# Two linear-attention and MLP layers on one core: the mask of K'V in pieces, b1 turned by DMA, and a new order of operations

## The chip, the cores and the metric

The kernel runs on one core of a Trainium2 chip. Its time is device time of one execution in microseconds (us). It was run 12 times; the median is compared. One execution was also recorded by the hardware profiler, and the profile and the trace are of that one. The engines are called as the profile calls them: PE (TensorE: matmuls; PEld are its weight loads), DVE (VectorE), ACT (ScalarE), POOL (GpSimd) and SP (SyncE, which here only issues DMAs).

## What is computed

x has 2048 tokens of width 512. Two kinds of block alternate, A, B, A, B, each fed with a layernorm of x and added to x; both A blocks share their weights, and so do both B blocks.

```python
def A(x, wqkv, wo):                  # linear attention, 32 heads of 16
    q, k, v = heads(x @ wqkv)
    phi = lambda t: where(t > 0, t + 1, exp(t)) + 1e-6
    kv  = einsum("bhsd,bhse->bhde", phi(k), v)
    z   = phi(k).sum(s)
    o   = einsum(phi(q), kv) / (einsum(phi(q), z) + 1e-6)
    return o @ wo

def B(x, w1, b1, w2, b2):            # MLP, 512 -> 1792 -> 512
    h = gelu(layernorm(x) @ w1 + b1)
    return h @ w2 + b2

for _ in range(2):
    x = x + A(layernorm(x), wqkv, wo)
    x = x + B(layernorm(x), w1, b1, w2, b2)
```

The layernorm has no scale or shift. Inputs, weights and the output are bf16; the kernel keeps x in fp32 in SBUF from the first residual add to the last.

## The kernel before

**Tiles.** The tokens are 16 tiles of 128, in 4 chunks of 4 tiles. A layer, counted from 0 to 1, is one A and one B block. An operation is named by its kind, its layer and its tile or chunk: K0_8 is the key matmul of tile 8 in layer 0.

**The stages of a layer.** For every tile, `norm` (L569) takes bn_stats and bn_aggr on DVE (L573, L575), the power -1/2 on POOL (L585) and the normalised y on DVE (L598) or on ACT (L593, after a small product on POOL, L590). y is turned, features to partitions, in one of two ways: `transpose` (L604) has SP issue one DMA transpose of the 128x512 tile (L608); `transpose_pe` (L612) makes four transposes on PE (L621) and a copy out of PSUM on ACT (L631). A table WAY says which tiles go which way; tiles that it doesn't name go by DMA, and the y of layer 1's attention always does.

`attn_k` (L663) makes K of a tile with four matmuls (L672), and `phi` (L639) its exp on ACT (L642), relu on ACT (L653), a min on DVE (L655), and the sum on DVE or POOL (L659); a second form leaves out the relu and takes a maximum on DVE from PSUM (L646, L648). `attn_q` does this for Q of a chunk (L690 by token, L703 by feature), four groups of four matmuls. `attn_z` (L710) sums phi(K) over tokens by 16 small matmuls (L718).

V is not computed. By associativity K'V = (K' y) wv, so the kernel forms G = y' phi(K), 512x512: in layer 0 held in four PSUM banks over all tiles (`attn_g_held`, L737), in layer 1 chunk by chunk and added up in SBUF by DVE (`attn_g_chunk`, L769, L776 to L782). Then `attn_kv` (L785), once in a layer, is the junction between the key side and the query side:

- KV: 16 matmuls of 128 columns give the four diagonal 128x128 pieces of K'V in one PSUM bank (L792), from the copies of G in gtb (L753 on DVE, L750 on ACT).
- the mask: DVE multiplies the whole 128x512 bank with a 0/1 mask of 16x16 blocks into kvb (L809).
- M: four matmuls, each of one 128-column piece of kvb with wo (L813), whose results are copied to gtb, again by L753 and L750. They carry o and wo at once.

`attn_den` (L817) makes the denominators by a matmul (D, L859) and ln and exp(-x) on ACT (L861, L863), and scales phi(Q) on DVE or POOL (L867). Chunks 2 and 3 of layer 1 do it by token instead: a row product (L835), a sum over heads (L838), a reciprocal (L843), the scaling (L847), and a DMA transpose (L851). `attn_out` (L874) multiplies with gtb (WO, L883) and adds the residual (RA, DVE, L888). `mlp_front` (L891) norms and turns the tile again and adds b2 to x ahead of time (L900). `mlp_up` (L904) computes 14 feature groups of the chunk (W1, L915), with gelu and the bias b1c on ACT (L921); chunk 0 in two halves of 256 columns. `mlp_down` (L926) makes a tile's 14 matmuls in two runs of 7 (W2, L953), and DVE adds it to x (RB, L959) or, in layer 1, into the output buffer (L963), which SP stores (L965). The last tile is stored in two halves (L940 to L947).

**b1.** b1 is loaded as 14 rows of 128 into b1r (L987); a matmul with the identity turns it (L1007), and ACT copies it into b1c, one column for each feature group (L1009).

**What sets the order.** There is no loop on the chip. Each operation is put into a graph with what it reads, writes and holds, a duration, and a priority: a base by chunk and stage, plus a shift for its group from the table SHIFT. A list scheduler (L111) then plays the graph: of the operations whose inputs are ready within a window, an engine takes the one with the smallest priority number. Its durations decide the order alone; what comes out is a fixed list of instructions for each engine, with semaphore waits between engines where they are needed (`assign_waits`, L292). An engine works its list strictly in order, so an instruction that waits holds up all behind it, and SP's list holds all DMA transposes and output stores. Where a gelu follows an exp or ln in ACT's list, or the other way round, ACT loads its function table anew (L1085).

**Buffers.** PSUM has eight banks, given out by class: up-projection h at most 3 at once, down-projection and WO (w) 2, K 2, Q 2, G, KV and M together (g) 2, transposes and z (t) 2, D (n) 1. A tile's bank is free again when its last reader is done. The weights wv and wo are loaded by POOL's queue after tile 0's transpose, w1 and w2 after the last transposes of layer 0.

Of the kernel before, what the change touches and what calls it, by code (L numbers as in the profile page):

```python
# [6 lines left out]
BF16 = mybir.dt.bfloat16  # L7
# [284 lines left out]
def assign_waits(graph, order, sems, dma_sems):  # L292
# [10 lines left out]
    while len(done) < total:  # L303
# [45 lines left out]
    N_HALF=1, N_K=2, N_Q=2, P_Z0=5.39, N_PB=1, N_PT=8, P_DEN=-48.34, P_A2=-5.06, P_W1=49.73, P_W2=87.05,  # L349
    P_K=33.61, P_G=135.4, P_Q=207.59, STEP=5.63, A1_Q=118.84, A1_STEP=1.49, N_H=3, N_N=1, GAP=12.11,  # L350
    TABLE_PENALTY=11.0, WINDOW=97.32,
    SHIFT={
        "B00_0": -63.5, "B00_1": -8.1, "B00_2": 7.3, "B00_3": -93.5, "B01": 60.2, "B02": 12.9, "B03": 195.1,
        "B10_0": 6.1, "B10_1": -62.8, "B10_2": -11.2, "B10_3": 31.6, "B11": 42.0, "B12": 48.9, "B13": -60.8,
        "D00": -42.5, "D01": 23.0, "D02": 55.4, "D03": 24.7, "D10": -118.7, "D11": -103.1, "D12": 76.7,
        "D13": 90.0, "G00_0": -130.5, "G00_1": 65.4, "G00_2": -14.1, "G00_3": -19.5, "G01_0": 15.9,
        "G01_1": 32.9, "G01_2": 2.4, "G01_3": -18.4, "G02_0": 89.2, "G02_1": 11.0, "G02_2": 152.3,
        "G02_3": -18.7, "G03_0": 58.4, "G03_1": 74.1, "G03_2": 101.0, "G03_3": 281.4, "G10": -248.4,
        "G11": 5.3, "G12": 7.7, "G13": -15.3, "K00_0": -188.0, "K00_1": -66.0, "K00_2": -160.3,
        "K00_3": -101.8, "K01_0": -46.3, "K01_1": -84.0, "K01_2": -197.2, "K01_3": -13.6, "K02_0": 7.6,  # L360
        "K02_1": 18.1, "K02_2": 72.9, "K02_3": 2.3, "K03_0": -251.2, "K03_1": 0.9, "K03_2": 2.8,
        "K03_3": 76.6, "K10": 72.4, "K11": 2.0, "K12": 63.8, "K13": -58.7, "N00_0": -106.8, "N00_1": -194.3,
        "N00_2": -80.9, "N00_3": -49.7, "N01_0": -228.4, "N01_1": -16.6, "N01_2": -83.5, "N01_3": -64.6,
        "N02_0": -10.3, "N02_1": -11.4, "N02_2": -8.6, "N02_3": -0.6, "N03_1": 96.6, "N03_2": -8.3,
        "N03_3": 103.1, "N10": 6.8, "N11": -48.1, "N12": -72.3, "N13": -200.4, "O00_0": -264.0, "O00_1": 4.0,
        "O00_2": 1.2, "O00_3": 41.0, "O01": -60.1, "O02": -3.5, "O03": 43.5, "O10_0": 86.0, "O10_1": -1.6,
        "O10_2": 9.3, "O10_3": -188.8, "O11": -55.5, "O12": 209.8, "O13": 11.7, "Q00": 5.8, "Q01": -60.9,
        "Q02": 42.5, "Q03": 86.6, "Q10": 16.5, "Q11": -39.1, "Q12": 237.5, "Q13": 105.1, "U00_0": -36.4,
        "U00_1": -3.8, "U01": 7.7, "U02": -47.6, "U03": -113.5, "U10_0": 2.5, "U10_1": -172.4, "U11": 40.1,
        "U12": -58.4, "U13": 102.3, "V0": 2.2, "V1": 30.4, "W00": 0.8, "W01": 86.3, "W02": 7.8, "W03": -45.0,  # L370
        "W10": -2.9, "W11": 295.4, "W12": 166.9, "W13": 260.2, "Z00": 6.3, "Z01": 37.9, "Z02": 87.6,
        "Z10": -7.3, "Z11": -9.0, "Z12": -118.0, "Z13": -122.1, "b1": 69.7,
    },
    WAY={
        "TA0_0": "pe", "TA0_1": "pe", "TA0_2": "pe", "TA0_3": "pe", "TA0_4": "pe", "TA0_5": "pe",
        "TA0_6": "pe", "TA0_7": "pe", "TB0_0": "dma", "TB0_1": "pe", "TB0_2": "dma", "TB0_3": "dma",
        "TB1_0": "pe", "TB1_1": "pe", "TB1_2": "dma", "TB1_3": "dma", "b20_0": "dve", "b20_1": "dve",
        "b20_10": "dve", "b20_11": "pool", "b20_12": "pool", "b20_13": "pool", "b20_15": "pool",
        "b20_2": "pool", "b20_3": "dve", "b20_4": "dve", "b20_5": "dve", "b20_6": "dve", "b20_7": "dve",
        "b20_8": "dve", "b20_9": "pool", "b21_0": "pool", "b21_1": "pool", "b21_10": "pool", "b21_11": "dve",  # L380
        "b21_12": "pool", "b21_13": "pool", "b21_14": "dve", "b21_15": "pool", "b21_2": "pool",
        "b21_3": "dve", "b21_4": "pool", "b21_5": "pool", "b21_6": "dve", "b21_7": "dve", "b21_8": "dve",
        "b21_9": "pool", "cpg0_0": "dve", "cpg0_1": "dve", "cpg0_2": "dve", "cpg0_3": "act", "cpg1_0": "act",
        "cpg1_1": "act", "cpg1_2": "act", "cpg1_3": "dve", "cpm0_0": "act", "cpm0_1": "dve", "cpm0_2": "dve",
        "cpm0_3": "act", "cpm1_0": "dve", "cpm1_1": "dve", "cpm1_2": "dve", "cpm1_3": "act", "den1_2": "tok",
        "den1_3": "tok", "normA0_0": "dve", "normA0_1": "dve", "normA0_10": "dve", "normA0_11": "act",
        "normA0_12": "dve", "normA0_13": "dve", "normA0_14": "dve", "normA0_15": "dve", "normA0_2": "dve",
        "normA0_3": "dve", "normA0_4": "dve", "normA0_5": "dve", "normA0_6": "dve", "normA0_7": "dve",
        "normA0_8": "dve", "normA0_9": "dve", "normA1_0": "act", "normA1_1": "dve", "normA1_10": "act",
        "normA1_11": "dve", "normA1_12": "dve", "normA1_13": "act", "normA1_14": "act", "normA1_15": "dve",  # L390
# [758 lines left out]
```

## Time and profile before

| what | value |
|---|---|
| median of 12 runs | 337.22 us (336.42 to 338.06) |
| the profiled execution's own time | 336.8 us |
| its span in the trace | 335.0 us |
| PE busy | 323.6 us, 1752 instructions |
| ACT busy | 222.8 us, 368 instructions |
| DVE busy | 203.0 us, 439 instructions |
| POOL busy | 140.0 us, 224 instructions |
| DMA transposes of y, issue to landing | 53, median 2.5 us |
| function table loads on ACT | 22 x 1.283 us |

The span is what the engines' records cover; the execution's own time is 1.8 us longer. A busy time is the union of an engine's records, so one matmul of 512 columns shows as 379 ns though the next one starts 216 ns after it. A group's line gives the source line, the engine, the operation and its shapes, the count, and after the bar the busy time and the mean of one in ns; after the second bar the time that the engine stood idle just before these instructions, and what ended most of it. The chain of work is followed back from the last instruction, each step to what released it.

### The profile page before, as it was taken

The numbers are of one execution on the slowest core, as the hardware profiler recorded it, in microseconds if no ns is written. First come the engines' busy times: TensorE is split into PE (matmuls) and PEld (weight loads), VectorE is DVE, ScalarE is ACT, GpSimd is POOL, SyncE is SP. The second block draws the span as 40 slices with busy tenths as digits, with TensorE's granted clock in tenths as the row PEclk, the third lists the DMA queues.
The fourth block names the chain that finished last, engine by engine and source line by source line (L and its number), as shares of the span: only waits on it lengthen the run. The fifth ranks groups of instructions, "written<-read, shape, count | busy, mean of one in ns | idle before, by whom it ended". The sixth has DMA issues, their size and how long they took to land.

```text
span 335.0 us, 4817 instructions
## 1 busy us (share of the span) xinstructions
PE 323.6 (97%) x1752; PEld 160.8 (48%) x1783; DVE 203.0 (61%) x439; ACT 222.8 (67%) x368; POOL 140.0 (42%) x224
## 2 busy tenths in 40 slices
PE   7889998999999999999999999999999999999996
PEld 2444443576444444444444444458644444444444
DVE  6987757985791017696305789699787593430122
ACT  3876899879569998642984398969916738327000
POOL 6653444466462012668303352678648271300000
PEclk9999999999999999999999999999999999999999
DMA  8733740022122000123200110003133412120011
GB/s 270 247 57 71 277 165 0 18 50 47 31 61 36 0 0 2 31 47 65 47 0 2 31 31 4 1 0 65 33 85 72 49 32 63 31 49 0 31 39 58
DMA packets 40068, 18.41 MB, mean 55 GB/s; under 512 B 33708, under 2 KB 39084, under 8 KB 40044
## 3 DMA queue, kind: packets, MB, share of 16 engines
q1 hardware_dynamic: 36476, 10.89, 15.7%
q0 software_dynamic: 1056, 4.72, 4.0%
q10 hardware_dynamic: 2512, 2.49, 2.3%
q8 instruction: 14, 0.23, 0.3%
q14 instruction: 10, 0.08, 0.1%
HBM read 8.00 MB, written 2.10 MB: 30 GB/s over the span
## 4 chain that ended last, share of the span: by engine, by line
PE 86%; DVE 6%; DMA 4%; POOL 1%; issue 1%; ACT 1%; POOLq 0%
PE ps L915 29%; PE ps L953 25%; PE ps L672 7%; PE ps L883 7%; PE ps L703 5%; PE ps L769 4%; PE ps L737 4%; DMA t<-yb 3%; PE ps L690 2%; DVE xsb L888 1%; PE ps L859 1%; DVE stats L573 1%; DMA t<-in_A_x_dram 1%; DVE gtb L753 1%; DVE yb L598 1%
## 5 line engine op out<-in xcount | busy, mean ns | idle before, releaser
L915 PE MATMUL ps<-t,w 128*128 128x512 bf16 (+1 forms) x555 | 99.5, 336 | 0.5 <-DMA t<-yb 0.3
L921 ACT ACTIVATE gT<-ps,b1c 128x512 bf16<-128x512 f32 (+1 forms) x140 | 79.3, 604 | 31.0 <-PE ps L915 30.8
L953 PE MATMUL ps<-w,gT 128*128 128x512 bf16 x424 | 96.9, 379 | 0.6
L915 PEld LDWEIGHTS ps<-t,w 128*128 128x128 bf16 x560 | 54.4, 98 | 43.9 <-DMA t<-yb 0.8
L953 PEld LDWEIGHTS ps<-w,gT 128*128 128x128 bf16 x434 | 42.2, 98 | 49.5
L642 ACT ACTIVATE eb<-ps 128x512 bf16<-128x512 f32 x64 | 38.6, 612 | 24.2 <-PE ps L672 16.1
L655 DVE TENSOR_SCALAR eb<-eb 128x512 bf16<-128x512 bf16 x56 | 18.2, 333 | 41.4 <-ACT eb L642 41.0
L585 POOL TENSOR_TENSOR rstd<-veps,neghalf 128x1 f32<-128x1 f32 x64 | 38.7, 605 | 7.2 <-DVE veps L583 2.1
L653 ACT ACTIVATE rb<-ps 128x512 bf16<-128x512 f32 x56 | 34.1, 616 | 0.0
L672 PE MATMUL ps<-wqkv,t 128*128 128x512 bf16 x123 | 31.3, 379 | 2.1 <-DMA t<-yb 1.8
L573 DVE BATCH_NORM_STATS2 stats<-xsb 128x6 f32<-128x512 f32 x48 | 32.6, 683 | 0.5
L883 PE MATMUL ps<-gtb,t 128*128 128x512 bf16 x123 | 30.8, 379 | 1.4 <-DVE gtb L753 1.0
L593 ACT ACTIVATE yb<-xsb,nmr,rstd 128x512 bf16<-128x512 f32 x20 | 16.2, 811 | 23.8 <-POOL nmr L590 23.0
L659 POOL TENSOR_TENSOR pkb<-eb,rb 128x512 bf16<-128x512 bf16 x11 | 12.8, 1170 | 35.9 <-ACT rb L653 18.3
L963 DVE TENSOR_TENSOR outb<-ps,xsb 128x512 bf16<-128x512 f32 x15 | 10.3, 684 | 28.7 <-PE ps L953 28.7
L1085 ACT ACT_TABLE_LOAD x21 | 26.9, 1283 | 0.4
L598 DVE TENSOR_SCALAR yb<-xsb,mv,rstd 128x512 bf16<-128x512 f32 x28 | 20.0, 717 | 8.5 <-POOL rstd L585 8.1
L867 POOL TENSOR_TENSOR t<-t,lr 128x512 bf16<-128x512 bf16 x14 | 16.3, 1165 | 20.6 <-ACT lr L863 20.5
L703 PE MATMUL ps<-t,wqkv 128*128 128x512 bf16 x92 | 23.1, 379 | 0.3
L900 POOL TENSOR_TENSOR xsb<-xsb,b2b 128x512 f32<-128x512 f32 x17 | 20.2, 1196 | 6.5 <-DVE yb L598 4.6
L883 PEld LDWEIGHTS ps<-gtb,t 128*128 128x128 bf16 x128 | 12.3, 98 | 16.7 <-DVE gtb L753 2.4
L672 PEld LDWEIGHTS ps<-wqkv,t 128*128 128x128 bf16 x128 | 12.0, 98 | 16.3 <-ACT rb L653 1.1
(82 smaller groups left out, 349.4 us busy)
## 6 DMA issues: line engine op xcount, KB each, us to landing
w<-in_B_w_dram POOLq DMA_DIRECT2D x4, 896.0 KB, 8.5
out_dram<-outb SPq DMA_DIRECT2D x15, 128.0 KB, 1.7
t<-in_A_x_dram ACTq DMA_DIRECT2D x3, 512.0 KB, 7.9
t<-yb SPq DMA_TRANSPOSE x53, 2.5
wqkv<-in_A_wqkv_dram SPq DMA_DIRECT2D x1, 512.0 KB, 5.2
wqkv<-in_A_wqkv_dram ACTq DMA_DIRECT2D x1, 512.0 KB, 7.0
wqkv<-in_A_wqkv_dram POOLq DMA_DIRECT2D x1, 512.0 KB, 6.8
wo<-in_A_wo_dram POOLq DMA_DIRECT2D x1, 512.0 KB, 6.3
```

The costliest lines, as they stand in the source:

```text
L573: G.op("dve", lambda e: e.bn_stats(stats[:, s.slot, :], src()), 620, reads=src_keys, writes=[k + "s"], tiles=[s, *src_tiles], prio=prio, n ...
L585: G.op("pool", lambda e: e.tensor_tensor(rstd[:, s.slot:s.slot + 1], veps[:, s.slot:s.slot + 1], neghalf[:], op=ALU.pow), 570, reads=[k + ...
L598: G.op("dve", lambda e: e.tensor_scalar(yb[:, y.slot, :], src(), mv[:, s.slot, 0:1], rstd[:, s.slot:s.slot + 1], op0=ALU.subtract, op1=ALU ...
L642: G.op("act", lambda e: e.activation(eb[:, et.slot, :], bank(bt), ACT.Exp), 478, reads=[src_key], writes=[f"e{tag}"], tiles=[bt, et], prio ...
L653: G.op("act", lambda e: e.activation(rb[:, rt.slot, :], bank(bt), ACT.Relu), 478, reads=[src_key], writes=[f"r{tag}"], tiles=[bt, rt], pri ...
L672: ins = e.matmul(bank(b), lhsT=yTa(yT)[:, dt, k * P:(k + 1) * P], rhs=wqkv[:, dt, D:2 * D], start=(dt == 0), stop=(dt == DT - 1))
L703: ins = e.matmul(bank(b), lhsT=wqkv[:, dt, kt * P:(kt + 1) * P], rhs=yTa(yT)[:, dt, :], start=(dt == 0), stop=(dt == DT - 1))
L883: ins = e.matmul(bank(wb), lhsT=yTa(pq)[:, kt, k * P:(k + 1) * P], rhs=gtb[:, kt, :], start=(kt == 0), stop=(kt == DT - 1))
L915: ins = e.matmul(bank(b, n), lhsT=w1[:, dt, ft * P:(ft + 1) * P], rhs=yTa(yT)[:, dt, k0 * P:k1 * P], start=(dt == 0), stop=(dt == DT - 1))
L921: G.op("act", lambda e, ft=ft, b=b, k0=k0, k1=k1, n=n: e.activation(gT[:, g.slot, ft * 512 + k0 * P:ft * 512 + k1 * P], bank(b, n), ACT.Ge ...
L953: ins = e.matmul(bank(b), lhsT=gT[:, g.slot, ft * 512 + k * P:ft * 512 + (k + 1) * P], rhs=w2[:, ft, :], start=(ft == 0), stop=(ft == FT - 1))
L1085: e.preload_act_table_set(sets[table])
```

## The change

Four edits:

1. `attn_kv` masks K'V in four instructions of 128 columns instead of one of 512, and each M matmul reads only its own piece.
2. b1 is turned by a DMA transpose that SP issues (from a 16-row b1r, which POOL clears first, into b1t) instead of a matmul; ACT then copies from b1t in SBUF instead of from PSUM. The transpose waits for b1's load and for the last transpose of layer 0.
3. A shift may be given to a single operation by its name, besides its group, and the tables of shifts and ways, the window, the penalty for a table change and the numbers of PSUM banks are new: K may hold 3 banks instead of 2, h 4 instead of 3, D 2 instead of 1. Of the transposes, tile 6 of layer 0 goes from PE to DMA and tile 11 from DMA to PE; of the MLP's, layer 0's tile 2 goes to PE and layer 1's tile 1 to DMA.
4. The scheduler's latency for a DMA transpose is 1300 instead of 1000; as every number of the scheduler it reaches the chip only through the order.

Entries of WAY whose names the program never asks for ("TA1_..", "tc_..") do nothing. The diff, with the tables cut to their first entries:

```diff
 CONF = dict(
-    N_HALF=1, N_K=2, N_Q=2, P_Z0=5.39, N_PB=1, N_PT=8, P_DEN=-48.34, P_A2=-5.06, P_W1=49.73, P_W2=87.05,
-    P_K=33.61, P_G=135.4, P_Q=207.59, STEP=5.63, A1_Q=118.84, A1_STEP=1.49, N_H=3, N_N=1, GAP=12.11,
-    TABLE_PENALTY=11.0, WINDOW=97.32,
+    N_HALF=1, N_K=3, N_Q=2, P_Z0=6.99, N_PB=1, N_PT=8, P_DEN=-45.12, P_A2=-16.36, P_W1=58.86, P_W2=84.95,
+    P_K=47.92, P_G=125.74, P_Q=226.77, STEP=5.92, A1_Q=51.41, A1_STEP=3.23, N_H=4, N_N=2, GAP=9.92,
+    TABLE_PENALTY=0.77, WINDOW=100.11,
     SHIFT={
-        "B00_0": -63.5, "B00_1": -8.1, "B00_2": 7.3, "B00_3": -93.5, "B01": 60.2, "B02": 12.9, "B03": 195.1,
+        "B00_0": -215.0, "B00_1": -89.8, "B00_2": -26.6, "B00_3": 14.5, "B01": 170.5, "B02": 2.6,
...
     WAY={
-        "TA0_0": "pe", "TA0_1": "pe", "TA0_2": "pe", "TA0_3": "pe", "TA0_4": "pe", "TA0_5": "pe",
-        "TA0_6": "pe", "TA0_7": "pe", "TB0_0": "dma", "TB0_1": "pe", "TB0_2": "dma", "TB0_3": "dma",
-        "TB1_0": "pe", "TB1_1": "pe", "TB1_2": "dma", "TB1_3": "dma", "b20_0": "dve", "b20_1": "dve",
+        "TA0_0": "pe", "TA0_1": "pe", "TA0_10": "dma", "TA0_11": "pe", "TA0_12": "dma", "TA0_13": "dma",
+        "TA0_14": "dma", "TA0_15": "dma", "TA0_2": "pe", "TA0_3": "pe", "TA0_4": "pe", "TA0_5": "pe",
+        "TA0_6": "dma", "TA0_7": "pe", "TA0_8": "dma", "TA0_9": "dma", "TA1_0": "dma", "TA1_1": "dma",
...
-        b1r = SB("b1r", [FT, P], BF16)
+        b1r = SB("b1r", [16, P], BF16)
+        b1t = SB("b1t", [P, 16], BF16)
...
-                        name=name, lat=1000.0 if transpose else DMA_LAT + (1500.0 if eng == "pool" else 0.0), sem=sem, nbytes=busy, after=after)
+                        name=name, lat=1300.0 if transpose else DMA_LAT + (1500.0 if eng == "pool" else 0.0), sem=sem, nbytes=busy, after=after)
...
+        G.op("pool", lambda e: e.memset(b1r[:], 0.0), 100, writes=["b1r"], prio=-100)
...
-            G.op("dve", lambda e: e.tensor_tensor(kvb[:], bank(b), bdmask[:], op=ALU.mult), 600,
-                 reads=[f"kv{L}", "bdmask"], writes=["kvb"], tiles=[b], prio=prio, name=f"kvm{L}", lat=40)
+            for kt in range(DT):
+                cs = slice(kt * P, (kt + 1) * P)
+                G.op("dve", lambda e, cs=cs: e.tensor_tensor(kvb[:, cs], bank(b)[:, cs], bdmask[:, cs], op=ALU.mult), 200,
+                     reads=[f"kv{L}", "bdmask"], writes=[("kvb", kt)], tiles=[b], prio=prio, name=f"kvm{L}_{kt}", lat=90)
             for kt in range(DT):
                 mb = Tile(psum, f"m{L}_{kt}", "g")
                 G.op("pe", lambda e, kt=kt, mb=mb: e.matmul(bank(mb), lhsT=kvb[:, kt * P:(kt + 1) * P], rhs=wo[:, kt, :], start=True, stop=True),
-                     MM, reads=["kvb", "wo"], writes=[f"mp{L}_{kt}"], tiles=[mb], prio=prio, name=f"M{L}_{kt}", lat=MM_DRAIN)
+                     MM, reads=[("kvb", kt), "wo"], writes=[f"mp{L}_{kt}"], tiles=[mb], prio=prio, name=f"M{L}_{kt}", lat=MM_DRAIN)
...
-                    dma("sp", lambda e: e.dma_start(b1r[:], B_b1.rearrange("(ft p) -> ft p", p=P)), ["b1r"], prio=-80, name="b1", kb=4, after=[tr])
+                    dma("sp", lambda e: e.dma_start(b1r[0:FT, :], B_b1.rearrange("(ft p) -> ft p", p=P)), ["b1r"], prio=-80, name="b1", kb=4,
+                        after=[tr])
...
-        b1b = Tile(psum, "b1", "g")
-        G.op("pe", lambda e: e.matmul(bank(b1b)[:, 0:FT], lhsT=b1r[:, :], rhs=idp[0:FT, 0:FT], start=True, stop=True), 200,
-             reads=["b1r", f"id{P}"], writes=["b1p"], tiles=[b1b], prio=-20, name="b1T", after=trs[-1:], lat=MM_DRAIN)
-        G.op("act", lambda e: e.activation(b1c[:], bank(b1b)[:, 0:FT], ACT.Copy), 200, reads=["b1p"], writes=["b1c"], tiles=[b1b],
-             prio=-20, name="b1c")
+        dma("sp", lambda e: e.dma_start_transpose(b1t[:], b1r[:]), ["b1t"], reads=["b1r"], prio=-20, name="Tb1", after=trs[-1:], transpose=True)
+        G.op("act", lambda e: e.activation(b1c[:], b1t[:, 0:FT], ACT.Copy), 200, reads=["b1t"], writes=["b1c"], prio=-20, name="b1c")
...
-            o.prio += cf["SHIFT"].get(o.grp, 0.0)
+            o.prio = round(o.prio + cf["SHIFT"].get(o.grp, 0.0) + cf["SHIFT"].get(o.name, 0.0), 2)
```

## The prediction, made before the changed kernel ran

> **What bounds the kernel now.** I read the page's sums and slices first, then the waits of TensorE, then the chain of work in order of time, then the groups by line, and last the order in which each engine's instructions stand, before and after.
>
> ```profile
> span 335.0 us, 4817 instructions
> ...
> PE 323.6 (97%) x1752; PEld 160.8 (48%) x1783; DVE 203.0 (61%) x439; ACT 222.8 (67%) x368; POOL 140.0 (42%) x224
> ...
> PE   7889998999999999999999999999999999999996
> ...
> PEclk9999999999999999999999999999999999999999
> ```
>
> TensorE is busy in 323.6 of 335.0 us at a full clock; no slice after the fifth falls under 9 until the last. So 11.4 us are idle, and no more can come from order. The first matmul starts at 1.51 us and the last ends at 332.5 (the chain shows a result leaving VectorE from 332.55 on), so about 1.5 + 2.5 us are start and end, which no edit touches. What is left is 7.4 us.
>
> ```profile
> PE ps L672 <- DMA t<-yb: 1.8, 2, 1.3
> PE ps L557 <- DVE onesm L522: 1.5, 1, 1.5
> PE ps L621 <- DVE yb L598: 1.4, 2, 0.9
> PE ps L883 <- DVE gtb L753: 1.0, 2, 0.7
> PE ps L813 <- DVE kvb L809: 0.6, 1, 0.6
> PE ps L859 <- DVE t L659: 0.3, 1, 0.3
> PE ps L915 <- DMA t<-yb: 0.3, 1, 0.3
> ```
>
> Columns: who waited, for what; us in total, times, longest. The waits have names: a key matmul (L672) for a DMA transpose, twice; the two first transposes on TensorE (L621); and the junction where K'V is masked (kvb, L809) and multiplied by wo into gtb (L753). The chain says when:
>
> ```profile
> 18.43 4.42 DMA t<-yb
> ...
> 52.25 0.69 DVE kvb L809
> ...
> 53.74 1.21 DVE gtb L753 x2
> ...
> 194.58 2.39 DMA t<-yb
> ...
> 293.90 3.61 DMA t<-yb
> ```
>
> Columns: start, length. Each is a stretch in which the chain left TensorE. In the timeline of TensorE's starts they cost, by start-to-start time less 0.216 us a matmul (the pace inside every block): 1.42 at 21.8 (K of tile 8, layer 0); 0.19 + 0.73 + 0.91 + 0.30 from 51.4 to 57.0 (first junction); 0.50 at 135 (D of chunk 3); 0.69 at 196 (K of tile 14, layer 1); 0.25 + 0.38 and small change, 0.85, from 211 to 216 (second junction); 0.45 at 297 (up-projection of chunk 2, layer 1). The head, 5.1 to 9.9, holds 2.1 more, and b1's small matmul 0.2. Sum 8.3: the 7.4, and edges that the busy time counts as work.
>
> ```profile
> L1085 ACT ACT_TABLE_LOAD x21 | 26.9, 1283 | 0.4
> L753 DVE TENSOR_SCALAR gtb<-ps 128x512 bf16<-128x512 f32 x8 | 5.1, 683 | 1.3 <-PE ps L737 0.7 <-PE ps L813 0.6
> L809 DVE TENSOR_TENSOR kvb<-ps,bdmask 128x512 bf16<-128x512 f32 x2 | 1.4, 692 | 1.6 <-PE ps L792 1.6
> L1007 PE MATMUL ps<-idp,b1r 14*128 14x14 bf16 x1 | 0.2, 178 | 0.0
> ```
>
> **What the Trainium skill says.** "VectorE: DVE Perf Modes", section on the TRN2 errata, prices a PSUM-source VectorE operation at 120 + columns cycles of 0.96 GHz: 658 ns for 512 columns (trace: 692 for L809, near), 258 for 128. Its section "The three transpose paths" gives 1309 ns for a 128x128 DMA transpose against 390 on TensorE; here a transpose of a whole 128x512 tile holds SP's queue 1.19 to 1.27 us and lands after a median 2.5, so the measured pair is used. "ScalarE: Activation LUTs", section "What ACT_TABLE_LOAD costs", says 1283 ns for each load: exactly the row. "Perfetto Trace Analysis", section "Optimizing Scalar/DVE Operations", holds that breaking up instructions may let work complete sooner when they cause bubbles on another engine: L809 before L813 is such a bubble of 0.6.
>
> **The change, part by part.** Work on TensorE is the same but for one matmul: 8 + 3 tile transposes on TensorE in both orders (tiles 6 and layer 1's tile 1 go to DMA, tile 11 and layer 0's second-half tile 2 come back), no other matmul added. So the whole account is in waits.
>
> *b1 by DMA.* L1007 goes: start-to-start around it was 0.42 instead of 0.22, so -0.2. Added: a POOL memset of 16x128 while POOL idles before 1.5 us (nothing); one DMA transpose on SP, unpriced in this small shape, between 0 and 1.3 us of queue, taken as 1.25. Behind it stand the transposes of tiles 14 and 13; by my count their keys are wanted 1.5 and 0.9 us after they land, so hidden; worth 0.4 if that cover is gone. On ScalarE b1c now waits for it: it should land near 31 us and ScalarE comes to b1c at 31.6; behind it waits the exp of tile 9, whose matmul ends later still. Bounds 0 to +1.2; I take 0.
>
> *Mask in pieces.* Four pieces of 128 columns; between L945's 424 ns for 256 columns and L809's 692 for 512 the slope is 268 per 256, so 290 ns for 128, spaced 0.2. First junction by the new order: G15 part 0, Q, KV0, G15 parts 1 to 3, D, KV1, KV2, D, KV3, Q, M0, M1, D, M2, M3, Q, WO. From the end of part 0: KV0 waits 0.07; KV1 waits for its copy (part 1 at 1.37 + 0.2 + 0.68) 0.28; KV2 for the next copy, 0.6 later, 0.38; M0 follows a Q of 0.86 us that covers the first piece; M1 needs KV's bank, freed by the last piece, 0.06; M2 waits for ScalarE's copy of M0 (0.6), 0.36; M3 for VectorE's copy of M1, 0.15; WO finds all four. Sum 1.3 against 2.13: -0.8. Second junction, same way, with class g's two banks: about 0.2 + 0.1 + 0.4; but then VectorE has two phi, one row product (L835, 0.68), one head reduction (L838, 0.67) and one scaling ahead of the first residual add, which before came at once. WO tiles have two banks, freed by those adds: waits of 0.25, 0.1, 0.1 and 0.45. Sum 1.6 against 0.85: +0.75.
>
> *Order: head.* The first DMA transpose is now tile 6, issued when its norm ends, near 11.7 instead of 18.4. At the 4.4 us that the first one took it lands at 16.1. The order wants it after G0 (ends at 11.85, as before), K4, G1, tile 3's transposes, G2, K3, tile 7's, Q: 11.85 + 5 x 0.86 + 2 x 0.22 + 0.4 of wait = 17.0, covered. Tile 8, issued near 15.4, lands by 18; K6, K7, G3, G4, a transpose and a z sum (0.38) later, at 21, it is wanted. The wait of 1.42 goes; tile 3's norm moves to ScalarE (0.8 us) ahead of two phi parts, so its copy ends near 15.0 and its key matmul waits 0.4; 0.2 for transposes shifted. Net -0.8.
>
> *Order: middle and end.* D of chunk 3 now comes with its Q long done: -0.5. The key of tile 15 (layer 1) stands 12 groups of 0.86 = 10.3 us after its down-projection; residual 0.7, stats 0.7, aggregation behind two accumulations, POOL's phi of 1.17 twice, norm, 2.5 for the DMA make 9.5: -0.7. Chunk 2 of layer 1 had 10.2 us from its last WO to its up-projection; it gets 15.5 (four down-projections of 3.03, four WO of 0.86): -0.45. Table loads: counting the switches in ScalarE's order gives 13 instead of 21, 8 x 1.283 = 10.3 us of ScalarE, which is idle a third of the time and waits for TensorE: nothing by itself.
>
> Sum: -0.2 - 0.8 + 0.75 - 0.8 - 0.5 - 0.7 - 0.45 = -2.7. A new order has waits that a count at known places misses; I add 0.5 for them (two of the sizes seen). Net -2.2 on the profiled execution's own 336.8 (span 335.0, 1.8 around it): 334.6. That execution lies 0.4 under the median 337.2, so 335.0 for a median; I write 334.9.
>
> **The rivals.**
> *Deeper.* The new order's waits are mostly filled and nothing is missed: the second junction is no worse than before (0 for +0.75), nothing is added (0 for 0.5), the head gains its whole 1.4: -2.7 - 0.75 - 0.6 = -4 and 333.1, in a range of 332.2 to 333.6. For: the sum of waits allows it. Against: the junction's bank limits are still there.
> *An exchange of waits.* Each wait taken is given back elsewhere, as every engine's list is new: 336.9. For: slack at tiles 13 and 15 is under a microsecond. Against: three of the taken waits have several us of new cover.
> *Slower: VectorE held up by POOL at the second junction.* At 193.08 one norm took 1.48 us, where the same at 222.40 took 0.54, while POOL ran 1.15 us operations; a phi at 196.10 took 1.13 instead of 0.42. Ahead of layer 1's first residual adds the new list has two min, two phi and soon the first norm on VectorE beside POOL's row product and scalings. If three lose 0.85 each, 2.6 us more pass before WO's banks come free, and tile 1, now turned by DMA (2.5) and no longer on TensorE, reaches the up-projection late by another 0.7. Then +0.75 + 3.3 stands against -3.4 and the 0.5: +1.1, 338.3. It decides from 2.2 us of extra wait there. Against: Q fillers of 0.86 stand between the WO.
>
> **How the numbers follow.** Forecast 0.52 (range 333.6 to 336.3), deeper 0.22, exchange 0.13, slower 0.13. About 0.2%, 0.7 us, is what a measurement of this kernel can tell from no change. Faster: the forecast but for 0.01, and deeper, and 0.02 of the exchange: 0.75; same 0.12; slower 0.13. The range for 8 in 10 takes in the deeper case to its lower end and reaches up through most of the exchange: 332.2 to 337.2.
>
> **What would show it.** Right: TensorE's waits after show no L672 for a DMA near 22 or 196 us, no key-value wait over 0.4, TensorE idle near 9 us, busy unchanged within 0.3, 13 table loads. The second junction should show more waits than before, ended by the residual adds. Wrong: a first DMA transpose that lands after 17 us while the weight loads still run (they end near 14.9); ScalarE idle before b1c; a wait of over 1 us before the up-projections, ended by a DMA transpose; norms of over 1 us ahead of layer 1's residual adds.

## The result, and the profile after

The changed kernel takes 332.99 us (median of 8 runs, 332.62 to 334.27) against 337.12 for the kernel before, measured beside it: a ratio of 0.9884, 95% interval 0.9875 to 0.9894, or 4.1 us less. The forecast was 334.9, with 333.6 to 336.3 as its own range; the time lies below that range and in the one of the rival called "deeper" (333.1, 332.2 to 333.6). The profiled execution has a span of 331.3 us for 335.0 before, so the two traces have 3.7 of the 4.1 us to explain.

The page of the kernel after: span, busy times, and from its fourth part the chain's shares by engine.

```profile
span 331.3 us, 4810 instructions
...
PE 323.8 (98%) x1750; PEld 161.4 (49%) x1782; DVE 206.8 (62%) x445; ACT 212.8 (64%) x361; POOL 139.8 (42%) x225
...
PE 94%; ACT 2%; DVE 2%; issue 1%; POOL 1%
```

PE does the same work (323.8 us busy for 323.6) in a shorter span: all that was won is idle time, 11.4 us before and 7.5 now. The chain that ended last runs over PE for 94% of the span, for 86% before, and no DMA is left in it. The waits of PE, after (who waited for what; us in total, times, longest):

```profile
PE ps L595 <- DVE onesm L559: 1.5, 1, 1.5
PE ps L659 <- DVE yb L636: 0.7, 1, 0.7
PE ps L756 <- DVE pkb L697: 0.3, 1, 0.3
PE ps L830 <- DVE gtb L791: 0.2, 1, 0.2
```

Lines stand some 38 to 40 higher than before (L672 is L710, L813 is L853, L883 is L923). The list has four entries where it had seven, and two of the four are the start and the first transposes. The waits for DMA transposes are gone, and so are those for the masked K'V and for the copies ahead of WO (before: 0.6 and 1.0). New are a short wait of the K'V matmuls (L830) for copies of G and the third entry: the z sum of chunk 2 waits for a phi. The timeline of DVE and POOL shows why (start, length, engine, line, operation):

```profile
35.89 1.56 DVE L684 TENSOR_SCALAR eb<-eb 128x512 bf16<-128x512 bf16 x1 [0.42 <-ACT eb L680]
...
36.12 1.17 POOL L697 TENSOR_TENSOR pkb<-eb,rb 128x512 bf16<-128x512 bf16 x1
```

DVE's operation (L684) takes 1.56 us beside POOL's phi, then DVE makes the last phi of the chunk; PE loses 0.50 at 38.2. The two junctions are best read in PE's timeline (start, length, line, instructions in a row). Before, the first one:

```profile
53.00 1.04 PE L813 MATMUL ps<-wo,kvb 128*128 128x512 bf16 x4 [0.57 <-DVE kvb L809]
53.87 0.38 PE L859 MATMUL ps<-t,zb 128*128 128x512 bf16 x1
55.00 2.86 PE L883 MATMUL ps<-gtb,t 128*128 128x512 bf16 x11 [0.74 <-DVE gtb L753]
```

and the second:

```profile
214.94 0.85 PE L883 MATMUL ps<-gtb,t 128*128 128x512 bf16 x2
216.00 1.47 PE L883 MATMUL ps<-gtb,t 128*128 128x512 bf16 x6 [0.21 <-DVE gtb L753]
```

After, both:

```profile
52.60 0.59 PE L853 MATMUL ps<-wo,kvb 128*128 128x512 bf16 x2
...
53.69 1.03 PE L741 MATMUL ps<-t,wqkv 128*128 128x512 bf16 x4
54.55 1.46 PE L923 MATMUL ps<-gtb,t 128*128 128x512 bf16 x6
...
213.23 0.81 PE L923 MATMUL ps<-gtb,t 128*128 128x512 bf16 x3
213.88 1.89 PE L728 MATMUL ps<-wqkv,t 128*128 128x512 bf16 x8
215.72 2.98 PE L923 MATMUL ps<-gtb,t 128*128 128x512 bf16 x13
```

At the first junction a group of Q (L741) stands between M (L853) and WO (L923), and another ahead of M: 53.69 to 54.55 is 4 x 0.216, so WO starts without a wait. The K'V matmuls before that still wait, 0.30 and 0.37, for copies, and 0.09 is lost twice. At the second, Q groups (L728) stand among the WO, and from 215.72 on thirteen WO matmuls run through. By the same count as in the prediction (start to start, less 0.216 a matmul) the first junction loses 0.85 us for 2.13 before, the second 0.16 for 0.85.

**One wait of before was counted too long.** The prediction has 1.42 us for the key of tile 8. The trace of before lacks the record of that key's first matmul: 1752 matmuls are recorded for 1783 weight loads, and here three matmuls stand beside four loads:

```profile
22.96 0.56 PEld L672 LDWEIGHTS ps<-wqkv,t 128*128 128x128 bf16 x4 [1.12 <-ACT rb L653]
...
23.21 0.81 PE L672 MATMUL ps<-wqkv,t 128*128 128x512 bf16 x3 [1.28 <-DMA t<-yb]
```

In the key matmuls of this trace whose records are whole, the second load starts within 0.01 us of the first matmul. Here it starts at 22.99, so the wait was 1.20 us, and the same wait is 1.13 to 1.29 in experiments 2, 3, 6 and 9, which keep this order. What follows counts with 1.20.

### The profile page after: what moved, and what is told of

Read it like the earlier page. It is cut to its first block, busy times and chain, and to the rows that moved or that the text cites. A ratio compares the mean times of both kernels' runs of the same rounds, so it can differ in the third digit from the quotient of the medians.

```text
span 331.3 us, 4810 instructions
## 1 busy us (share of the span) xinstructions
PE 323.8 (98%) x1750; PEld 161.4 (49%) x1782; DVE 206.8 (62%) x445; ACT 212.8 (64%) x361; POOL 139.8 (42%) x225
## 4 chain that ended last, share of the span: by engine, by line
PE 94%; ACT 2%; DVE 2%; issue 1%; POOL 1%
PE ps L955 29%; PE ps L993 28%; PE ps L923 8%; PE ps L710 7%; PE ps L741 6%; PE ps L807 4%; PE ps L775 3%; PE ps L728 2%; PE ps L595 1%; PE ps L899 1%; ACT eb L680 1%; PE ps L756 1%; PE ps L980 1%; PE ps L830 1%; PE ps L853 1%
## 5 line engine op out<-in xcount | busy, mean ns | idle before, releaser
L961 ACT ACTIVATE gT<-ps,b1c 128x512 bf16<-128x512 f32 (+1 forms) x140 | 80.2, 603 | 38.7 <-PE ps L955 38.5
L955 PE MATMUL ps<-t,w 128*128 128x512 bf16 (+1 forms) x551 | 98.5, 336 | 0.5
L691 ACT ACTIVATE rb<-ps 128x512 bf16<-128x512 f32 x55 | 33.2, 623 | 15.5 <-PE ps L710 12.4
L999 DVE TENSOR_TENSOR xsb<-ps,xsb 128x512 f32<-128x512 f32 x16 | 10.9, 682 | 39.0 <-PE ps L993 38.9
L710 PE MATMUL ps<-wqkv,t 128*128 128x512 bf16 x127 | 31.5, 379 | 0.4
L621 POOL TENSOR_SCALAR veps<-mv 128x1 f32<-128x1 f32 x29 | 7.8, 269 | 53.5 <-DVE mv L613 53.0
L923 PE MATMUL ps<-gtb,t 128*128 128x512 bf16 x126 | 29.9, 379 | 0.1
L907 POOL TENSOR_TENSOR t<-t,lr 128x512 bf16<-128x512 bf16 x15 | 18.1, 1214 | 16.5 <-ACT lr L903 16.5
L693 DVE TENSOR_SCALAR eb<-eb 128x512 bf16<-128x512 bf16 x55 | 20.1, 374 | 7.8 <-ACT eb L680 7.5
L741 PE MATMUL ps<-t,wqkv 128*128 128x512 bf16 x94 | 23.7, 379 | 0.1
L636 DVE TENSOR_SCALAR yb<-xsb,mv,rstd 128x512 bf16<-128x512 f32 x27 | 18.4, 682 | 7.8 <-POOL rstd L623 7.6
L923 PEld LDWEIGHTS ps<-gtb,t 128*128 128x128 bf16 x128 | 12.4, 98 | 15.7 <-DVE t L907 0.4
L710 PEld LDWEIGHTS ps<-wqkv,t 128*128 128x128 bf16 x128 | 12.2, 98 | 14.9 <-ACT t L669 0.9
```

What stands on the lines that cost most here:

```text
L691: G.op("act", lambda e: e.activation(rb[:, rt.slot, :], bank(bt), ACT.Relu), 478, reads=[src_key], writes=[f"r{tag}"], tiles=[bt, rt], pri ...
L693: G.op("dve", lambda e: e.tensor_scalar(eb[:, et.slot, :], eb[:, et.slot, :], 1.0, 1e-6, op0=ALU.min, op1=ALU.add), 210, reads=[f"e{tag}"] ...
L710: ins = e.matmul(bank(b), lhsT=yTa(yT)[:, dt, k * P:(k + 1) * P], rhs=wqkv[:, dt, D:2 * D], start=(dt == 0), stop=(dt == DT - 1))
L741: ins = e.matmul(bank(b), lhsT=wqkv[:, dt, kt * P:(kt + 1) * P], rhs=yTa(yT)[:, dt, :], start=(dt == 0), stop=(dt == DT - 1))
L923: ins = e.matmul(bank(wb), lhsT=yTa(pq)[:, kt, k * P:(k + 1) * P], rhs=gtb[:, kt, :], start=(kt == 0), stop=(kt == DT - 1))
L955: ins = e.matmul(bank(b, n), lhsT=w1[:, dt, ft * P:(ft + 1) * P], rhs=yTa(yT)[:, dt, k0 * P:k1 * P], start=(dt == 0), stop=(dt == DT - 1))
```

## The experiments

All are measured beside the kernel before. Wherever a kernel says "order kept", the order of every engine's list was taken from the named kernel by one line in the scheduler, and each edit changes no more than what is shown:

```diff
-                for o in released[e]:
+                for o in [o for o in released[e] if (o.name or "-") == ORDER[e][len(self.order[e])]]:
```

**1. Edit 3 alone.** The order of after, with the mask whole and b1 turned on PE, as before. The tables of ways are those of after too; besides the transposes, they give 64 operations that both kernels have to another engine.

```diff
-            for kt in range(DT):
-                cs = slice(kt * P, (kt + 1) * P)
...
+            G.op("dve", lambda e: e.tensor_tensor(kvb[:], bank(b), bdmask[:], op=ALU.mult), 600,
...
-        dma("sp", lambda e: e.dma_start_transpose(b1t[:], b1r[:]), ["b1t"], reads=["b1r"], prio=-20, name="Tb1", after=trs[-1:], transpose=True)
+        G.op("pe", lambda e: e.matmul(bank(b1b)[:, 0:FT], lhsT=b1r[:, :], rhs=idp[0:FT, 0:FT], start=True, stop=True), 200,
```

> The changed kernel's order, with the mask whole again in one instruction and b1 turned on TensorE again: edit 3 alone. My theory: the order is nearly the whole gain, because a query group of 0.86 us stands between the last KV matmul and the first M in the new order and covers a whole mask (0.2 + 0.69). Only b1's 0.2 comes back: 3.9 us under the kernel before, ratio 0.988 to 0.990, no wait of L853's successor for the mask over 0.1. Rival, that the pieces are needed: 0.8 to 1.3 us come back, ratio 0.991 to 0.993, and the M matmuls wait for the mask in both layers.

Measured: 333.20 us, ratio 0.9886 (0.9869 to 0.9903), the kernel after within 0.2. b1's matmul stands at 36.7 and costs PE 0.18; the two places of the mask lose 0.09 each. So edit 3, the new order with its ways, is the whole gain but for about 0.2 us; how much of it the other engines for those 64 operations give was not separated from the order. (41 PSUM tiles lie in other banks than after; experiment 7 shows why that has to be said.)

**2. The mask in pieces alone.** The order of before, the mask cut as in the diff.

> The kernel before, its order kept operation for operation, with the mask in four pieces: edit 1 alone. My theory: M waits 0.4 less in layer 0, but the four pieces hold VectorE 0.8 us instead of 0.6, so that the copies of M behind them come 0.2 later and WO waits that much longer, having waited for them anyway: within 0.3 us of the kernel before. Rival, that the pieces are a gain by themselves: 0.4 to 0.8 us faster.

Measured: 337.09, ratio 0.9999 (0.9990 to 1.0008): nothing. M's wait at the first junction fell from 0.73 to 0.33, and WO's rose from 0.91 to 1.20. But here the scheduler had also given 20 tiles other banks, among them WO's first. Experiment 9 does this cleanly.

**3. b1 by DMA alone,** ahead of all other transposes. It is the rival to my reading of the 4.42 us that the first DMA transpose took: if the first use is slow, b1 now pays for it.

```diff
-        dma("sp", lambda e: e.dma_start_transpose(b1t[:], b1r[:]), ["b1t"], reads=["b1r"], prio=-20, name="Tb1", after=trs[-1:], transpose=True)
+        dma("sp", lambda e: e.dma_start_transpose(b1t[:], b1r[:]), ["b1t"], reads=["b1r"], prio=-20, name="Tb1", transpose=True)
```

> The kernel before in its own order, with b1 turned by DMA, as the very first DMA transpose (right behind b2's load, without waiting for the last transpose of layer 0). It tells why the first DMA transpose took 4.4 us before. My theory now: a 16 KB instruction fetch at 19.3 us fell on it, so the key matmul of tile 8 still waits about 1.4 and the kernel gains only b1's 0.2. Rival, a cost of first use: the b1 transpose pays it, tile 8's transpose holds SP's queue 1.25 instead of 2.48, its wait shrinks to 0.2 or less, and the kernel is 1.2 to 1.5 us faster.

Measured: 337.03, ratio 0.9993 (0.9985 to 1.0002). b1's transpose went out at 12.1 us without harm, and tile 8's, now the second, still held SP for 2.69 us and its key waited 1.29. So the long hold is no price of first use (experiment 12 goes on from here). The time prices b1's edit only roughly, between 0.5 us and nothing: 154 PSUM tiles lie in other banks than before, PE has a new wait of 0.47 for a gelu at 66.3, and WO's 0.30 at 57 is gone. The 0.2 is read from the matmul itself (experiment 1).

**4. Every table load doubled,** in the kernel after: 13 more loads of 1.283 us, 16.7 us more of ACT, to see if ACT's time is as free as the prediction took it.

```diff
+                    e.preload_act_table_set(sets["gelu" if table == "gelu" else "exp"])
                     table = o.table
```

> The changed kernel with every load of ScalarE's function table preceded by a second one: about 13 more loads, 16 us more of ScalarE. My theory: ScalarE is not the bound and the eight loads saved gave nothing; within 0.5 us of the changed kernel (ratio to before 0.988 to 0.990). Rival, that the saved loads (10.3 us) gave a part of the gain: at least 1 us of it is lost again and TensorE waits for ScalarE.

Measured: 341.55, ratio 1.0142 (1.0120 to 1.0165): 8.5 us slower than after. My expectation failed. The largest of PE's waits in this kernel:

```profile
PE ps L955 <- ACT gT L961: 4.8, 4, 2.2
```

The up-projection waits for the gelu that empties its bank, at 66.4, 105.0, 166.3 and 233.6, by 0.7 to 2.4 us. Two things are possible: the single loads cost something too, or ACT's slack at these places lies between one load and two. Experiments 6, 7 and 10 decide.

**5. Two banks at the junctions.** The kernel after, with what the prediction had assumed put in by hand: M2 and M3 wait for the copies of M0 and M1, and layer 1's WO tiles 2 to 7 for the residual add that empties one of two banks.

```diff
-                     MM, reads=[("kvb", kt), "wo"], writes=[f"mp{L}_{kt}"], tiles=[mb], prio=prio, name=f"M{L}_{kt}", lat=MM_DRAIN)
+                     MM, reads=[("kvb", kt), "wo"], writes=[f"mp{L}_{kt}"], tiles=[mb], prio=prio, name=f"M{L}_{kt}", lat=MM_DRAIN, after=cps[kt - 2:kt - 1] if kt > 1 else ())
...
+        two = {2: 0, 3: 1, 4: 2, 5: 4, 6: 3, 7: 5}
...
-                     name=f"WO{L}_{st}_{part[0]}", lat=MM_DRAIN, n=len(part))
+                     name=f"WO{L}_{st}_{part[0]}", lat=MM_DRAIN, n=len(part),
+                     after=[ras[L, two[st]]] if L and st in two else ())
```

> The changed kernel with the waits that the prediction counted for PSUM banks, put in by hand: M2 and M3 of both layers wait for the copies of M0 and M1, and WO of tiles 2 to 7 in layer 1 for the residual adds that would free one of two banks. Order and work are the same. My theory: the durations of the prediction's count were right and only its rule for the banks was wrong, so the waits come back as counted, 0.5 for M in each layer and about 0.9 for WO: 1.2 to 2.2 us over the changed kernel, ratio to before 0.992 to 0.995. Rival: the adds and copies come early enough on VectorE that even two banks cost nothing (within 0.4 us of the changed kernel), so that the size of VectorE's work was misjudged, not the banks.

Measured: 334.52, ratio 0.9919 (0.9896 to 0.9941): 1.2 us slower than after by the ratios, 1.5 by the medians. The banks and the order are those of after. One of its new waits, M (here L854) for a copy:

```profile
PE ps L854 <- DVE gtb L791: 0.4, 1, 0.4
```

M now loses 0.42 and 0.10 at 53 us, where the prediction had 0.57 for it, and 0.52 at 213; WO loses 0.17, 0.17, 0.09 and 0.24 from 217 to 223. The second junction's part is 1.2, where the prediction had 1.6. These waits are real once the banks are two; in the kernel after they are not.

**6 and 7. No table loads, before and after.** gelu is replaced by exp, which changes the computation, so that ACT loads nothing.

```diff
-ACT.Gelu_apprx_tanh, bias=
+ACT.Exp, bias=
...
-lat=110, table="gelu")
+lat=110, table="exp")
```

> The kernel before in its own order with gelu replaced by exp in the up-projection, so that ScalarE needs no second function table and makes none of the 21 loads; this changes what is computed. My theory: no wait of TensorE there was ended by ScalarE's gelu, so all 21 loads (26.9 us) were hidden and it gains less than 0.5 us. Rival, that saved loads are part of the change's gain: 8 of 21 loads for at least 1 us of it would make this one 1.5 us or more faster than the kernel before.

> The changed kernel with gelu replaced by exp, so that the 13 loads go; this changes what is computed. My theory: no wait of TensorE is ended by ScalarE there either, so it stays within 0.4 us of the changed kernel, though one more load at each place cost 8.5 us: the order has just as much slack as its own loads need. Rival: the loads still cost a part, 1 us or more faster.

Measured: before without loads 337.08, ratio 0.9998 (0.9984 to 1.0011). 166 PSUM tiles lay in other banks, but the trace shows the waits of before, each in its place. So all of its loads were hidden, to within the 0.5 us of the interval. After without loads 333.77, ratio 0.9903 (0.9875 to 0.9930), 0.8 us slower than with them. Its one new wait, of 0.9 us at 213 and for a copy of M, has nothing to do with gelu: as the scheduler counts the loads, 71 tiles had got other banks. This run settles nothing; run 10 repeats it with the banks of after.

**8. The two waits that are left,** in the kernel after: phi of tile 15 made by DVE instead of POOL, and the last three parts of G15 ahead of the Q group and the first K'V that stood before them.

```diff
-"phik0_15": "pool",
...
-G0_15_0 Q0_2_1 KV0_0 G0_15_1 G0_15_2 G0_15_3
+G0_15_0 G0_15_1 G0_15_2 G0_15_3 Q0_2_1 KV0_0
```

> The changed kernel with two operations moved: phi of tile 15 (layer 0) from POOL to VectorE, since a VectorE min of 0.3 us took 1.56 beside it and a z sum waited 0.5 for what followed; and the last three parts of G of tile 15 ahead of the query group before them, so that their copies are done when KV needs them (waits of 0.30 and 0.37). My theory: both waits go, 0.7 to 1.2 us under the changed kernel, ratio to before 0.9845 to 0.987. Rival: the waits move on to the next operations of VectorE, within 0.3 us of the changed kernel.

Measured: 332.13, ratio 0.9855 (0.9828 to 0.9881), about 0.9 us less than after and the fastest of all; with five runs the two intervals just touch (after: 0.9875 to 0.9894). The 0.50 at 38 us and the 0.30 and 0.37 at 50 are gone; 0.46 and 0.13 are new. Four of its five runs lie at 332.05 to 332.19, one at 333.26, and that one is the profiled one:

```profile
PE ps L955 <- DMA t<-yb: 0.9, 1, 0.9
```

Here the up-projection waits for layer 1's tile 1, which the change had given to DMA; its transpose went out at 220.9 and was not there at 224. The kernel after shows no such wait in its trace, but one of its runs (334.27) is 1.3 us above the others too.

**9. The mask in pieces alone, with the banks of before.** As experiment 2, and every PSUM tile in the bank that it has in the kernel before.

```diff
-        for b in allowed:
+        for b in (SLOT[t.name],) if t.name in SLOT else allowed:
```

> The kernel before, its order and every PSUM bank kept as they were, with K'V masked in four pieces and nothing else (in the earlier run of this edit the planner had given 20 tiles other banks). My theory: four pieces hold VectorE for about 0.8 us instead of 0.7, M0 starts 0.4 earlier at each junction, and the output projection behind it still waits for the same copies, so the wait moves there: M's wait 0.6 to 0.2-0.3, the output projection's up by 0.1 to 0.4, time within 0.3 us of before. Rival: in the earlier run only the other banks hid the gain, and with the old banks the pieces give 0.4 to 0.8 us.

Measured: 337.15, ratio 1.0000 (0.9992 to 1.0008). DVE's timeline in this kernel at the first junction:

```profile
52.77 0.88 DVE L811 TENSOR_TENSOR kvb<-ps,bdmask 128x128 bf16<-128x128 f32 x4 [1.15 <-PE ps L792]
53.57 0.68 DVE L869 TENSOR_TENSOR t<-t,lr 128x512 bf16<-128x512 bf16 x1
54.17 0.29 DVE L655 TENSOR_SCALAR eb<-eb 128x512 bf16<-128x512 bf16 x1
54.37 1.28 DVE L753 TENSOR_SCALAR gtb<-ps 128x512 bf16<-128x512 f32 x2
```

Four pieces start 0.2 apart, so the next instruction starts 0.80 after the mask instead of 0.60. A scaling and a min stand behind the mask in DVE's list, and only then come the copies that WO waits for. M may start 0.40 sooner; the copies start 0.2 later, and WO waits 1.50 where it waited 0.91. The wait moved one step on and grew by that 0.2. "Perfetto Trace Analysis", section "Optimizing Scalar/DVE Operations", says that breaking up instructions that cause bubbles may let work complete sooner; here M did, and nothing was won, because the same engine owed the next step as well.

**10. No table loads, after, with the banks of after.**

> The kernel after, order and PSUM banks kept, gelu replaced by exp so that no table is loaded at all (this changes the computation). In the earlier run of this edit 71 tiles had other banks and one wait of 0.9 us at the second junction was new. My theory: that wait came from the banks, and the 13 loads of the kernel after stand in time in which ScalarE waits for TensorE: within 0.3 us of the kernel after (332.7 to 333.3), no wait over 0.6 at the second junction. Rival: doubling the loads cost 8.5 us, so some single loads stand on the path too: 1 us or more faster than the kernel after, below 332.0.

Measured: 332.87, ratio 0.9877 (0.9864 to 0.9890), the kernel after within 0.12, and no wait at the second junction. So the 13 loads cost nothing where they are (within the interval, 0.4 us), and the prediction's "nothing by itself" holds. Experiment 4 shows how near the edge they are: one more load at the same places costs 8.5 / 13 = 0.65 us on average.

**11. One piece of the new order in the old one:** the key of tile 8 behind two gate groups, banks kept.

```diff
-Z0_0 K0_8 G0_4_0 K0_9 G0_5_0 Z0_1
+Z0_0 G0_4_0 G0_5_0 K0_8 K0_9 Z0_1
```

> The kernel before, banks kept, with one piece of the new order: the key of tile 8 (layer 0) stands behind the held gate groups of tiles 4 and 5 instead of ahead of them. My theory: the wait of 1.3-1.4 us for tile 8's DMA transpose is covered by two groups of 0.86, the tiles behind are late enough for nothing to take its place, and 1.0 to 1.4 us come off: 335.7 to 336.2. Rival: DMA transposes leave SP one in about 1.25 us, so tile 9's or tile 14's key, or the phi of tile 8 that the z sum needs, is late next, and less than 0.5 us comes off.

Measured: 337.08, ratio 0.9998 (0.9988 to 1.0008). My expectation failed and the rival's time came true, though at other tiles than it named. PE's waits for keys:

```profile
PE ps L672 <- DMA t<-yb: 0.5, 1, 0.5
PE ps L672 <- DVE eb L646: 0.4, 1, 0.4
```

Tile 8's wait of 1.20 is gone; the DMA wait that is left is that of tile 15 at 197. In its place the second gate group loses 0.21 at 23.2, and the keys of tiles 11 and 12 lose 0.24 and 0.59 from 29.9 to 31.6, the latter for DVE (L646), which reads its bank late. About 0.15 of the 1.20 is left. The starts of the matmuls say the same: at 10.1 us, ahead of the edit, they lie 0.57 behind those of before (a slower first stretch), from 32 us on 0.43. Here a wait that was filled in one place was not won, because operations behind it were as late. In the kernel after it is won: PE has no wait of 0.06 or more from 15.4 to 38.2.

**12. A spare transpose.** The kernel before, banks kept, with one more DMA transpose of tile 8 just ahead of its own, into a buffer that nobody reads.

```diff
+                    if st == 8:
+                        dma("sp", lambda e, y=y: e.dma_start_transpose(scr[:].rearrange("p (d s) -> p d s", d=DT), yb[:, y.slot, :]), ["scr"],
+                            tiles=[y], reads=[ykey], prio=pr, name="TX", transpose=True)
```

> The kernel before, banks kept, with one more DMA transpose of tile 8 into a buffer that nobody reads, issued on SP just ahead of tile 8's own. My theory: it is the time and not the tile that makes a transpose hold SP's queue for 2.5 us; a 16 KB packet of queue q8 passes near 19-20 us. So the spare one, issued near 18.4, holds SP 1.9 to 2.7 us, tile 8's own then holds 1.2 to 1.3 and its key waits 0.3 to 1.0 us longer than before, 337.5 to 338.2. Rival: the long hold belongs to tile 8's own transpose (its data, its place in the list): the spare one takes 1.2, its own again 2.4 or more, the key waits 1.2 us longer or more, 338.3 or above.

Measured: 337.78, ratio 1.0027 (1.0015 to 1.0039). SP's queue in this kernel:

```profile
19.00 2.46 SPq L987 DMA_TRANSPOSE scr<-yb  x1
21.51 5.20 SPq L609 DMA_TRANSPOSE t<-yb  x4
```

The spare one holds the queue for 2.46, and the four behind it, tile 8's first, for 1.25 to 1.27 each. So the long hold goes with the time and not with the tile. Nor does it go with the first transpose of this shape: in the kernel after that one, issued at 12.04, held the queue for 1.30. What follows the hold is another matter: the first transpose of this shape lands 1.94 to 2.57 after its hold in the traces of before, after and experiments 3 and 12, and those behind it after about 1.2. Some 0.7 us of tile 8's late landing may thus go with being first; no run separates that. The key of tile 8 waits 1.74 instead of 1.20, and the median is 0.64 longer.

## Why the prediction was right, and where it was not

Direction and range held, and so did the mechanism in the main: the work on PE stayed, the waits went, and edit 3 did it. The size did not, -2.2 us forecast and -4.1 measured, and one step of the mechanism failed. By the prediction's own steps (us; measured in the traces as it was counted there):

| step | forecast | measured |
|---|---|---|
| b1 by DMA | -0.2 | -0.2 (0.18 in experiment 1) |
| first junction | -0.8 (2.13 to 1.3) | -1.3 (to 0.85) |
| second junction | +0.75 (0.85 to 1.6) | -0.7 (to 0.16) |
| head | -0.8 | -0.5: tile 8's -1.20, tile 3's key +0.22, the first stretch +0.44 |
| D of chunk 3 | -0.5 | -0.5 |
| key of tile 15, layer 1 (the list of waits calls it 14) | -0.7 | -0.7 |
| up-projection of chunk 2, layer 1 | -0.45 | -0.45 |
| waits not foreseen | +0.5 | +0.5 (z sum at 38.2) |
| sum | -2.2 | -3.85; the span fell by 3.7 |

The measured steps make 0.15 more than the span shows; that remainder is in small edges that I did not place. The first stretch is no work of the change: kernels with the old order have it slow too (see the last section). Without it the steps make -4.3, near the -4.1 of the medians.

Two agreements are luck. The 0.5 for waits not foreseen was an allowance, and one wait of that size came. And "deeper" has the right time by another account: it left the second junction as it was and had no new wait, where the second junction gained 0.7 and 0.5 was new. Of the signs of being right, the keys without a wait for DMA at 22 and 196, the K'V waits under 0.4, the unchanged busy time and the 13 loads came; TensorE's idle time is 7.5 and not near 9, and the second junction shows fewer waits than before, none ended by an add.

**The step that failed** is the one on the junctions: "with class g's two banks" for M, and "WO tiles have two banks, freed by those adds". The forecast of DVE's work ahead of the first add was right: two phi, a row product, a head reduction and a scaling stand there, and the add comes at 216.50:

```profile
213.91 0.42 DVE L697 TENSOR_TENSOR t<-eb,rb 128x512 bf16<-128x512 bf16 x1
214.36 0.69 DVE L875 TENSOR_TENSOR lr<-t,zrow 128x512 f32<-128x512 bf16 x1
214.97 0.69 DVE L907 TENSOR_TENSOR t<-t,lr 128x512 bf16<-128x512 bf16 x1
215.57 0.68 DVE L878 TENSOR_REDUCE rd<-lr 128x32 f32<-128x512 f32 x1
216.17 0.41 DVE L697 TENSOR_TENSOR t<-eb,rb 128x512 bf16<-128x512 bf16 x1
216.50 1.28 DVE L928 TENSOR_TENSOR xsb<-ps,xsb 128x512 f32<-128x512 f32 x2
```

But no matmul waited for the adds. The number in a bank class limits how many tiles the scheduler holds at once while it plays the graph, and a tile counts until its last reader has been placed. It does not tie the third tile to the bank of the first. In `take` (L269) a tile gets whichever allowed bank is free earliest, and a wait arises only on the readers of that bank. In the schedule after, M0 to M3 of layer 1 lie in banks 7, 1, 2 and 7, and the first WO tiles in 4, 3, 5 and 4: M2 has a bank of its own and needs no copy to be done, and the third WO needs no add; M3 and the fourth WO do share a bank with the first, which was free by then. At the first junction M0 to M3 lie in four banks (2, 3, 4 and 7), and the 0.36 and 0.15 that the prediction had for M2 and M3 did not come. Experiment 5 puts the assumed waits back and returns 1.2 to 1.5 of the 1.9 us by which the two junction steps were off.

The same rule makes two entries of the change idle once the order is given: scheduled with two banks for K and three for h, the new order gives every one of 341 PSUM tiles the same bank, so the same program (worked out from the schedule). They can matter only to which order the scheduler finds.

**The other points.** Table loads: nothing, as said (experiment 10), with less slack than I had thought (experiment 4). The mask in pieces: the prediction gave it no price apart from the order; alone it is worth nothing (experiment 9). Its price of 290 ns a piece, spaced 0.2, is what the trace shows (281 and 0.2); the estimate of 258 from "VectorE: DVE Perf Modes", section on the TRN2 errata, is a little short. The slower rival, DVE held up by POOL ahead of layer 1's adds, did not come: the two phi ahead of the adds took 0.42 and 0.41. It did come in small at 35.89, as the z sum's 0.5. "Exchange of waits" is how the single edits of experiments 9 and 11 behave, not the change as a whole.

**What stays open.** Why the new order keeps what experiment 11 loses was not split further; that would take lists changed for several engines together. How much comes from the order and how much from the other engines for 64 operations is open too.

## What to carry to other kernels

A limit in a planner is not a wait on the chip: before pricing a buffer's turn-round, look up which slot each tile got and whose readers that slot had. Where several engines are each nearly late, filling one wait can give the time to the next one (1.20 us filled, nothing gained in the time); look at what stands behind it. Two other small moves kept 0.9 us (experiment 8). A wait is read from the first record behind it, so make sure that this record is there (1.42 was 1.20). Test slack at two sizes: loads that cost nothing when taken away cost 8.5 us when doubled.

## What the runs showed of the hardware

**DMA transposes are stretched at certain times.** A 128x512 transpose holds SP's queue for 1.19 to 1.32 us as a rule. All those that held it for over 1.35 us in the traces of before (four), after (two) and experiment 3 (four) overlap a packet of 16,384 bytes on queue q8, which the page lists as of kind "instruction": 14 such packets in an execution, of 0.9 to 1.5 us each. In before one starts at 19.30, under tile 8's transpose (hold 2.48, landing after 4.42); in experiment 12 at 19.77, under the spare one. In experiment 8's profile one starts at 222.94, between the issue of tile 1's transpose and the wait for it. The reverse does not hold: in experiment 12 the transpose issued at 241.21 held the queue for 1.23 and landed after 2.40, under a packet that ran until 242.03. And a landing can be late without such a packet: tile 6's in the kernel after, issued at 12.04, held 1.30 and landed after 3.86. That the packet causes the long hold is argued from the coincidence; no run took the packets away.

**An operation of DVE can take five times its time beside POOL:** L684 took 1.56 us at 35.89 while POOL ran a phi, where the nine of its line have a median of 0.294. "Perfetto Trace Analysis", section "Optimizing Scalar/DVE Operations", names a read port of SBUF that the two share and that a two-port operation of DVE holds as an exclusive lock; the trace agrees in that the two overlap from 36.12 on and DVE's ends 0.16 after POOL's, and does not show the port. In experiment 8, where that phi is on DVE and POOL runs none there, the same operation took 0.33 and the wait was gone.

**The start is not the same in each run.** PE's first matmuls of 512 columns start 0.427 us apart, twice the later 0.216: 7 of them in the profile of before, 11 of after, and 11 in that of experiment 9, which keeps the order of before. "TensorE: Matmul & The Clock Gate", section "What's actually happening", says that the count varies from run to run; the traces agree. With the waits for the first norms it moves the end of the first gate group: 11.85 before, 12.29 after, 12.44 in experiment 9. So the difference between before and after here is not the change's.
